# Cosine attention and an MLP mixer on one core: loading q and k of pairs 15 to 17 ahead of v of pairs 12 to 17, with the row transposes of u and the weight loads moved

## The chip, the cores and the metric

The kernel runs on one core of a Trainium2 chip. The metric is device time in microseconds (us). The engines are TensorE (PE in the profile; PEld are its weight loads), VectorE (DVE), ScalarE (ACT), GpSimd (POOL) and SyncE (SP), which here only issues DMAs.

## The reference

```python
batch, n_heads, seq, head_dim = (8, 12, 448, 64)
q_n = q / (np.linalg.norm(q, axis=-1, keepdims=True) + 1e-06)      # k_n likewise
scores = np.matmul(q_n, k_n.transpose(0, 1, 3, 2)) / tau            # tau = 0.1
attn = softmax(scores)
x = (attn @ v) as (8, 448, 768)                                     # heads side by side
h = np.maximum(x.T @ w_tok1, 0.0) @ w_tok2                          # w_tok1 448x256, w_tok2 256x448
u = x + h.T
h2 = np.maximum(u @ w_ch1, 0.0) @ w_ch2                             # w_ch1 768x1536, w_ch2 1536x768
return u + h2
```

Inputs and output are float32. The products are made in float16 with float32 sums.

## The kernel before, in words

**Units of work.** Two heads make a pair `p`; 6 pairs make a batch (`NPAIR`), so there are 48 pairs. Three pairs make a half `n` (`HP`), which is one load of q, of k and of v (576 KB each). The 448 rows are 384 main rows, three to a partition, and 64 rest rows. The rest rows (`xq`, `xk`, `xv`) are loaded for a whole batch in pieces of 256 bytes (192 KB for `xq`, twice 96 KB for `xk` and for `xv`).

**The path of a pair.** q and k are squared (`squares`, L176 on POOL or DVE, L174 on ACT), summed over the head (`sums`, L189, and `sums_x`, L193, on DVE), turned into reciprocal norms (`rnorms`, L197 to L200, on ACT) and scaled to float16 (`scaled`, L207, and `scaled_x`, L213 and L218, on POOL) into `kq`. PE transposes `kq` into `pst` (L239 to L244) for pairs below 15 and DVE copies it to `qk`; from pair 15 on (`DMA_FROM`) a transposing DMA does it (L261). PE makes the scores `psS` (L297) and `psX` (L304), ACT their exponentials `pt` (L298, L305), PE the product with v, `psO` (L318, L320), and DVE divides by the sums (L323, L324) into `x`. The token layer is `psR` (L338, relu on DVE L341) and `psU` (L357, with `x` added by PE at L362 or by DVE at L367); it gives a pair's 128 columns of u, transposed (`ut`). v is cast to float16 by `cast_v` (L164, L168).

**The channel layer.** When the sixth pair of a batch has been through the token layer, `ch_units` puts 12 units of the first product (`m_ch1`: six `psG` matmuls, L385, and a relu on ACT, L387) and 6 or 8 units of the second (`m_ch2`: twelve `psF` matmuls, L399, and on DVE the sum with u, L402) in a `queue`. `m_ch2` needs u with rows on partitions; `u_tpose` makes that by a transposing DMA for each pair (L376: `ur` from `ut`). `feed(budget, least)` takes units from the queue where the program calls it: it adds the budget to an account, takes units while the account covers half of the next one, and takes them against the account while less than `least` ns have been done. A unit's price in this account is its columns over 2.4.

**Order.** The whole order is written out by hand: a loop over slots `i`, one for each pair, issues loads, then scores, then sums and norms, scaling, squares, casts and weight loads, and then the rest of PE's work with calls of `feed` in between. The dictionaries `qk_at`, `v_at`, `x_at` (`xq`, `xk`), `xv_at` and `ut_at` say in which slot a load or a row transpose is issued; within a slot q and k come first, then `x`, v, `xv`, and then the transposes. All of these are issued by SP, one after the other; weights for the channel layer (`weights_ch1`, L154; `weights_ch2`, L158; 1152 KB each as float16) by POOL. Every engine works in order, so an instruction that waits holds all later ones of its engine. Slot 6 (`FIRST`) is the first slot after batch 0's attention; it also catches up two pairs of the token layer.

**Buffers.** `qm` and `km` have three tiles (halves), `vm` two, `xq`, `xk`, `xv` two (batches), the score tile `psS` two, the other PSUM tiles four in all, `ost` two, `ur` two. A load of half 5 into `qm` thus waits until pairs 6 to 8 (half 2) have been scaled.

Of the kernel before, what the change touches and what calls it, by code (L numbers as in the profile page):

```python
# [22 lines left out]
def kernel(  # L23
# [14 lines left out]
    B, H, S, E = q.shape  # L38
# [9 lines left out]
    DT = D // P  # L48
# [4 lines left out]
    NPAIR = H // 2  # L53
    NP_ALL = B * NPAIR
    HP = 3
    NHALF = 2 * B
# [48 lines left out]
    def load_q(n, g0=0, g1=6):  # L105
        nc.sync.dma_start(**main(qm, q, "qm", n, g0, g1))

    def load_k(n, g0=0, g1=6, eng=nc.sync):
        eng.dma_start(**main(km, k, "km", n, g0, g1))

    def load_v(n):
        nc.sync.dma_start(**main(vm, v, "vm", n, bufs=2))

    def load_xq(b, g0=0, g1=12):
        if b not in xq:
            xq[b] = qkv.tile([XR, H, E], FP32, name=f"xq_{b}", tag="xq", bufs=2)
        nc.sync.dma_start(out=xq[b][:, g0:g1], in_=q[b, g0:g1, SM:S].rearrange("g p e -> p g e"))  # L117
# [8 lines left out]
    def load_xk(b, g0=0, g1=12, eng=nc.sync):  # L126
        load_x2(xk, k, "xk", b, g0, g1, eng)

    def load_xv(b, g0=0, g1=12):
        load_x2(xv, v, "xv", b, g0, g1)  # L130
# [26 lines left out]
    def weights_ch2(i):  # L157
        nc.gpsimd.dma_start(out=wc2t[:, 6 * i:6 * i + 6, :],  # L158
                            in_=moe_w_ch2[768 * i:768 * (i + 1)].rearrange("(t p) d -> p t d", p=P))
# [89 lines left out]
    def tpose(p):  # L249
        pst = pst_tile(p)  # L250
        tpose_main(p, pst, 0)
        tpose_main(p, pst, 1)
        tpose_x(p, pst)
        return pst

    def qk_copy(p, pst):
        nc.vector.tensor_copy(out=qk_tile(p)[:, 0:P * 7 + XR], in_=pst[:, 0:P * 7 + XR])

    def dma_tpose(p):
        n, j = p // HP, p % HP  # L260
        nc.sync.dma_start_transpose(out=qk_tile(p)[:].rearrange("d (c s) -> d c s", c=8),  # L261
                                    in_=kqs[n % 2][:, j].rearrange("p a c e -> p (a c e)"))
# [66 lines left out]
    def x_tpose(p):  # L329
        xTs[p] = att.tile([P, (NC + 1) * P], FP16, name=f"xT_{p}", tag="xT")  # L330
        nc.sync.dma_start_transpose(out=xTs[p][:].rearrange("d (c s) -> d c s", c=NC + 1),
                                    in_=xs[p][:].rearrange("p c d -> p (c d)"))
# [37 lines left out]
    def u_tpose(p):  # L370
        b, dt = p // NPAIR, p % NPAIR
        odd = b % 2
        if b not in urt:
            urt[b] = mix.tile([P, DT, 4, P], FP16, name=f"ur16_{b}", tag="ur16")
        n, lo = NC + odd, SM * odd
        nc.sync.dma_start_transpose(out=urt[b][:, dt, 0:n], in_=pairt[b // 2][0][:, dt, lo:lo + P * n])  # L376
# [37 lines left out]
    def ns(cols, n=1):  # L414
        return n * cols / 2.4
# [6 lines left out]
    queue = []  # L422
    fed = [0.0]

    def feed(budget, least=0.0):
        fed[0] += budget
        done = 0.0
        while queue and (fed[0] > queue[0][0] / 2 or done < least):
            t, fn = queue.pop(0)
            fn()  # L430
            fed[0] -= t
            done += t

    def at(slots):
        got = {}
        for p, s in slots.items():
            got.setdefault(s, []).append(p)
        return got


    FIRST = NPAIR
# [8 lines left out]
            s = 1 + sq_slot[3 * n + (0 if c1 == 21 else 2)]  # L450
            rn_at.setdefault(s, []).append((n, c0, c1))
    sc_at = at({p: {7: 6}.get(p, p - 2 if p < DMA_FROM else p - 3) for p in range(3, NP_ALL)})
    early_qk = {2: 0, 3: 4, 4: 6, 5: 8}
    qk_at = at({n: early_qk.get(n, 3 * n - 8) for n in range(2, NHALF)})
    v_at = at({n: {2: 1, 3: 5}.get(n, 3 * n - 5) for n in range(2, NHALF)})
    x_at = at({b: {1: 0, 2: 6}.get(b, 6 * b - 8) for b in range(1, B)})
    xv_at = at({b: 6 * b - 5 for b in range(1, B)})
    cast_at = at({n: {1: 2, 2: 6}.get(n, 3 * n - 2) for n in range(1, NHALF)})
    tok_slot = {p: FIRST if p in (FIRST - 2, FIRST - 1) else p + 2 for p in range(NP_ALL)}
    tok_at = at(tok_slot)  # L460
    tok2_slot = {p: max(tok_slot[p] + (p in X_DMA), 3) for p in range(NP_ALL)}
    tok2_at = at(tok2_slot)
    ut_at = at({p: t + 1 for p, t in tok2_slot.items()})

    def norm_begin(p, eq, ek):
        squares(p, eq, ek)
# [3 lines left out]
    def norm_sums(p):  # L470
        sums(p)
        if p % HP == 0:
            sums_x(p // HP)
# [6 lines left out]
    with tc.manual_schedule():  # L480
# [77 lines left out]
        for i in range(NP_ALL + 2):  # L558
            for n in qk_at.get(i, ()):
                load_q(n)  # L560
                load_k(n)
            for b in x_at.get(i, ()):
                load_xq(b)
                load_xk(b)
            for n in v_at.get(i, ()):
                load_v(n)
            for b in xv_at.get(i, ()):
                load_xv(b)
            if DMA_FROM <= i + 2 < NP_ALL:
                dma_tpose(i + 2)  # L570
            if i - 2 in X_DMA:
                x_tpose(i - 2)
            for p in ut_at.get(i, ()):
                u_tpose(p)

            left = next((t + 1 - i for t in sorted(tok2_at) if t >= i + (i == FIRST) and
                         any(p % NPAIR == NPAIR - 1 for p in tok2_at[t])), 6)
            quota = max(sum(t for t, _ in queue) - 2000.0, 0.0) / (4 if FIRST <= i < FIRST + 3 else left)
            def next_qk(p):
                if p < min(DMA_FROM, NP_ALL):  # L580
                    qk_copy(p, tpose(p))

            def tok2(p):
                m_tok2(p)
                if p % NPAIR == NPAIR - 1:
                    queue.extend(ch_units(p // NPAIR))

            def norm_rn():
                for n, c0, c1 in rn_at.get(i, ()):
                    rnorms(n, c0, c1)  # L590

            if i == FIRST:
                m_tok1(i - 2)
                pv(i - 1, 0)
                pv(i - 1, 1)
                tok2(i - 2)
                m_tok1(i - 1)
                next_qk(i)
                tok2(i - 1)
                for p in sum_at[i]:  # L600
                    norm_sums(p)
                feed(0.0, 1000.0)
                score(i, 0)
                norm_rn()
                score(i, 1)
                feed(0.0, 2000.0)
            elif 0 < i < NP_ALL:
                score(i, 0, 2 if i < 4 else 0)
                score(i, 1)
            if i != FIRST:  # L610
                for p in sum_at.get(i, ()):
                    norm_sums(p)
                norm_rn()

            if i >= FIRST:
                for p in sc_at.get(i, ()):
                    norm_scale(p, nc.gpsimd)
            for p in sq_at.get(i, ()):
                norm_begin(p, nc.scalar if p < 18 else nc.gpsimd, nc.scalar if p == 3 else nc.vector if 9 <= p < 12 else nc.gpsimd)
            if i < FIRST:  # L620
                for p in sc_at.get(i, ()):
                    norm_scale(p, nc.gpsimd)
            for n in cast_at.get(i, ()):
                cast_v(n)
            if i in (2, 4):
                weights_ch1(i // 4)
            if i in (6, 7):
                weights_ch2(i - 6)

            if i < FIRST:  # L630
                if i:
                    pv(i - 1, 0)
                if i:
                    score(i, 2)
                    score_x(i)
                if i + 1 < FIRST:
                    next_qk(i + 1)
                for p in tok_at.get(i, ()):
                    m_tok1(p)
                if i:  # L640
                    pv(i - 1, 1)
                for p in tok2_at.get(i, ()):
                    tok2(p)
            elif i == FIRST:
                score(i, 2)
                score_x(i)
                feed(0.0, 1000.0)
                next_qk(i + 1)
                feed(0.0, 1000.0)
            else:  # L650
                feed(quota * 0.25)
                next_qk(i + 1)
                if i <= NP_ALL:
                    pv(i - 1, 0)
                for p in tok_at.get(i, ()):
                    m_tok1(p)
                feed(quota * 0.25, 400.0)
                if i < NP_ALL:
                    score(i, 2)
                    score_x(i)  # L660
                for p in tok2_at.get(i, ()):
                    tok2(p)
                feed(quota * 0.25)
                if i <= NP_ALL:
                    pv(i - 1, 1)
                feed(quota * 0.25)
            if i == 2:
                place_w2()
# [38 lines left out]
```

## Time and profile before

| | us |
|---|---|
| median of 5 runs | 414.63 |
| lowest, highest | 411.53, 2160.04 |
| the profiled execution's own time | 414.63 |
| its span, from first to last instruction | 412.8 |

Busy time in the span, by engine: PE 391.8 us, DVE 203.0, ACT 229.3, POOL 208.8. PE's time counts a matmul from its start to its modelled end, so a full PE is not PE at its peak: six psG matmuls in a row take 1.14 us in the chain of waits. PE's clock can be granted in part: the mean over the span was 0.98 of full speed.

Transfers: 67.51 MB in 137194 packets, of which 93184 are under 512 bytes (the rest rows and the transposes). SP's queue moved 61.36 MB of it, POOL's 5.18 MB. From its issue to its landing a load of q took 5.7 us in the median, of k 7.5, of v 7.1, a row transpose of u 2.8, half of a channel weight 13.1 to 13.4.

How to read it: a share of busy time is a mean over stages. The table by windows shows the stages, the timeline shows in brackets how long an engine sat idle before an instruction and what ended it, and SP's rows (SPq) are the time that SP needed to issue a DMA.

### The profile page before, as it was taken

The numbers are of one execution on the slowest core, as the hardware profiler recorded it, in microseconds if no ns is written. First come the engines' busy times: TensorE is split into PE (matmuls) and PEld (weight loads), VectorE is DVE, ScalarE is ACT, GpSimd is POOL, SyncE is SP. The second block draws the span as 40 slices with busy tenths as digits, with TensorE's granted clock in tenths as the row PEclk, the third lists the DMA queues.
The fourth block names the chain that finished last, engine by engine and source line by source line (L and its number), as shares of the span: only waits on it lengthen the run. The fifth ranks groups of instructions, "written<-read, shape, count | busy, mean of one in ns | idle before, by whom it ended". The sixth has DMA issues, their size and how long they took to land.

```text
span 412.8 us, 9115 instructions
## 1 busy us (share of the span) xinstructions
PE 391.8 (95%) x3646; PEld 227.2 (55%) x3646; DVE 203.0 (49%) x461; ACT 229.3 (56%) x415; POOL 208.8 (51%) x308
## 2 busy tenths in 40 slices
PE   7689989799999999999999998999999999999995
PEld 2356545466555564565555664555555565565562
DVE  5788656466544555445544555246453443243021
ACT  6997688654767446564666246564566435611400
POOL 5886477298193938576583908457491600000000
PEclk9899989899999999999999999899999999999998
DMA  8999999996997788989895898989782353013012
GB/s 219 272 234 202 231 232 189 257 179 203 174 229 109 218 149 220 206 188 197 232 191 74 235 131 218 179 150 235 171 151 49 87 146 65 15 51 104 2 75 77
DMA packets 137194, 67.51 MB, mean 164 GB/s; under 512 B 93184, under 2 KB 133568, under 8 KB 137152
## 3 DMA queue, kind: packets, MB, share of 16 engines
q1 hardware_dynamic: 132976, 61.36, 70.0%
q0 software_dynamic: 3632, 5.18, 7.4%
q8 instruction: 28, 0.46, 0.5%
q10 hardware_dynamic: 544, 0.39, 0.3%
q14 instruction: 14, 0.11, 0.1%
HBM read 43.38 MB, written 11.01 MB: 132 GB/s over the span
## 4 chain that ended last, share of the span: by engine, by line
PE 53%; POOL 19%; issue 12%; DMA 7%; SPq 4%; ACT 2%; DVE 2%; POOLq 0%; DVEq 0%; ACTq 0%
PE psF L399 18%; PE psG L385 16%; POOL kq L207 7%; POOL sq L176 6%; PE psO L318 5%; PE psS L297 4%; DMA xk<-in_k_dram 4%; PE psR L338 3%; DMA qm<-in_q_dram 3%; PE psU L357 3%; POOL sqx L176 2%; POOL kq L218 2%; PE psX L304 2%; SPq L117 2%; PE psO L320 1%
## 5 line engine op out<-in xcount | busy, mean ns | idle before, releaser
L298 ACT ACTIVATE pt<-psS 128x896 f16<-128x896 f32 x141 | 124.0, 914 | 73.3 <-PE psS L297 73.2
L385 PE MATMUL psG<-ut,wc1t 128*128 128x448 f16 x576 | 124.7, 358 | 0.0
L399 PE MATMUL psF<-wc2t,gt 128*128 128x384 f16 x672 | 118.0, 328 | 0.0
L387 ACT ACTIVATE gt<-psG 128x448 f16<-128x448 f32 x96 | 51.8, 544 | 77.8 <-PE psG L385 77.5
L207 POOL TENSOR_TENSOR kq<-km,rn 128x384 f16<-128x384 f32 x47 | 39.0, 830 | 101.5 <-ACT rn L200 90.3
L399 PEld LDWEIGHTS <-gt 128*128 128x128 f16 x672 | 63.8, 98 | 41.8 <-issue 3.8
L385 PEld LDWEIGHTS <-wc1t 128*128 128x128 f16 x576 | 53.2, 99 | 48.9 <-issue 8.3
L402 DVE TENSOR_TENSOR ost<-psF,ur 128x384 f32<-128x384 f32 x56 | 31.2, 558 | 84.1 <-PE psF L399 79.5
L318 PEld LDWEIGHTS <-pt 128*128 128x128 f16 x1152 | 52.7, 98 | 19.3 <-issue 8.5
L318 PE MATMUL psO<-vt,pt 128*128 128x65 f16 x1152 | 58.5, 195 | 2.8 <-ACT gt L387 2.8
L189 DVE TENSOR_REDUCE ssq<-sq 128x12 f32<-128x768 f32 (+1 forms) x49 | 45.1, 930 | 14.8 <-POOL sq L176 11.7
L297 PE MATMUL psS<-qk 64*128 64x448 f16 x282 | 44.4, 363 | 4.0 <-ACT pt L298 4.0
L324 DVE TENSOR_TENSOR x<-psO,rec 128x256 f16<-128x256 f32 x96 | 40.7, 424 | 3.3
L320 PE MATMUL psO<-vx,pt 128*128 128x130 f16 x192 | 42.3, 220 | 0.0
L323 DVE RECIPROCAL rec<-psO 128x4 f32<-128x4 f32 x96 | 17.1, 178 | 49.4 <-PE psO L320 49.1
L176 POOL TENSOR_TENSOR sq<-km 128x384 f32<-128x384 f32 x43 | 35.3, 823 | 11.6 <-DMA km<-in_k_dram 11.5
L207 POOL TENSOR_TENSOR kq<-qm,rn 128x384 f16<-128x384 f32 x47 | 38.9, 827 | 0.0
L338 PE MATMUL psR<-x,w1t 128*128 128x128 f16 x384 | 29.6, 220 | 0.1
L297 PEld LDWEIGHTS <-qk 64*128 64x128 f16 x282 | 10.7, 94 | 33.2 <-issue 29.5
L367 DVE TENSOR_TENSOR ut<-psU,xT 128x448 f16<-128x448 f32 (+2 forms) x39 | 17.6, 478 | 22.8 <-PE psU L357 17.1
L357 PE MATMUL psU<-w2t,r 128*128 128x448 f16 x96 | 26.0, 354 | 2.7 <-DVE x L324 2.6
L305 ACT ACTIVATE pt<-psX 128x448 f16<-128x448 f32 x48 | 26.0, 543 | 0.0
(75 smaller groups left out, 337.5 us busy)
## 6 DMA issues: line engine op xcount, KB each, us to landing
vm<-in_v_dram SPq DMA_DIRECT2D x16, 576.0 KB, 7.1
out_dram<-ost SPq DMA_DIRECT2D x24, 384.0 KB, 2.9
qm<-in_q_dram SPq DMA_DIRECT2D x15, 576.0 KB, 5.7
km<-in_k_dram SPq DMA_DIRECT2D x15, 576.0 KB, 7.5
wc1t<-in_moe_w_ch_dram POOLq DMA_DIRECT2D x2, 1152.0 KB, 13.4
wc2t<-in_moe_w_ch_dram POOLq DMA_DIRECT2D x2, 1152.0 KB, 13.1
out_dram<-ost SPq DMA_DIRECT2D x8, 192.0 KB, 3.0
xq<-in_q_dram SPq DMA_DIRECT2D x7, 192.0 KB, 8.7
```

The costliest lines, as they stand in the source:

```text
L176: eng.tensor_tensor(out=out, in0=src, in1=src, op=ALU.mult)
L189: nc.vector.tensor_reduce(out=ssqs[p // HP % 3][:, lo + 6 * a0:lo + 6 * a1], in_=sq[p][:, a0:a1].rearrange("p a g e -> p (a g) e"), axis=A ...
L207: eng.tensor_tensor(out=kqs[n % 2][:, j, a, 0:NC, :].rearrange("p c (g e) -> p g c e", g=2), in0=src, in1=_bcast_free(rn, E), op=ALU.mult)
L297: nc.tensor.matmul(psS[:, g, 0:S], qk[r, P * c:P * (c + 1)], qk[r, 512:512 + S], start=True, stop=True)
L298: nc.scalar.activation(out=pt[:, 2 * S * c:2 * S * (c + 1)].rearrange("p (g s) -> p g s", g=2), in_=psS[:, :, 0:S], func=AF.Exp, scale=inv ...
L318: nc.tensor.matmul(psO[:, mm, E1 * g:E1 * (g + 1)], pt[:, at:at + P], vt[:, 2 * j + g, c, 0:E1], start=(g == 0 and c == 0), stop=False)
L320: nc.tensor.matmul(psO[:, mm, :], pt[:, PX + lo:PX + lo + P], vx[:, j, 0:2 * E1], start=False, stop=True)
L324: nc.vector.tensor_tensor(out=xs[p][:, 2 * a:2 * a + 2, :].rearrange("p m (g e) -> p m g e", g=2), in0=o[:, :, :, 0:E], in1=_bcast_free(re ...
L338: nc.tensor.matmul(psR[:, tt, :], w1t[:, m, tt * P:(tt + 1) * P], xs[p][:, m, :], start=(m == 0), stop=(m == NC))
L385: nc.tensor.matmul(psG[:], wc1t[:, dt, ct * P:(ct + 1) * P], ut[:, dt, sp], start=(dt == 0), stop=(dt == DT - 1))
L387: nc.scalar.activation(out=gt[:, ct, sp], in_=psG[:], func=AF.Relu)
L399: nc.tensor.matmul(psF[:], gt[:, ct, lo:lo + P], wc2t[:, ct, dh * DH:(dh + 1) * DH], start=(ct == 0), stop=(ct == CT - 1))
```

## The change

Six edits, all of order:

- q and k of half 5 (pairs 15 to 17) are issued in slot 7 instead of 8; v of half 4 (pairs 12 to 14) in slot 9 instead of 7, of half 5 in slot 11 instead of 10.
- the rest rows of q and k of batch 3 in slot 11 instead of 10; those of v of batch 2 in slot 9 instead of 7.
- the row transposes of u: of batch 0, three in slot 8 and three in slot 9, instead of slots 4, 4, 5, 6, 7, 7; of batch 1, two each in slots 12, 13 and 14, instead of one each in slots 9 to 14. From batch 2 on they stay.
- the weights of the channel layer in slots 2, 5, 7 and 8 instead of 2, 4, 6 and 7.
- the budget of `feed` in slots 6 to 11: such that six units are left of the queue at slot 12, spread evenly.
- the last forced feed between the scores of slot 6: one unit (1000 ns) instead of two (2000 ns).

```diff
-    early_qk = {2: 0, 3: 4, 4: 6, 5: 8}
+    early_qk = {2: 0, 3: 4, 4: 6, 5: 7}
     qk_at = at({n: early_qk.get(n, 3 * n - 8) for n in range(2, NHALF)})
-    v_at = at({n: {2: 1, 3: 5}.get(n, 3 * n - 5) for n in range(2, NHALF)})
-    x_at = at({b: {1: 0, 2: 6}.get(b, 6 * b - 8) for b in range(1, B)})
-    xv_at = at({b: 6 * b - 5 for b in range(1, B)})
+    v_at = at({n: {2: 1, 3: 5, 4: 9, 5: 11}.get(n, 3 * n - 5) for n in range(2, NHALF)})
+    x_at = at({b: {1: 0, 2: 6, 3: 11}.get(b, 6 * b - 8) for b in range(1, B)})
+    xv_at = at({b: {2: 9}.get(b, 6 * b - 5) for b in range(1, B)})
...
-    ut_at = at({p: t + 1 for p, t in tok2_slot.items()})
+    ut_at = at({p: 8 + p // 3 if p < NPAIR else 12 + (p - NPAIR) // 2 if p < 2 * NPAIR else t + 1
+                for p, t in tok2_slot.items()})
...
-            quota = max(sum(t for t, _ in queue) - 2000.0, 0.0) / (4 if FIRST <= i < FIRST + 3 else left)
+            if FIRST <= i < 2 * NPAIR:
+                quota = max(len(queue) - 6, 0) * ns(S, DT) / (2 * NPAIR - i)
+            else:
+                quota = max(sum(t for t, _ in queue) - 2000.0, 0.0) / left
...
                 score(i, 1)
-                feed(0.0, 2000.0)
+                feed(0.0, 1000.0)
...
-            if i in (2, 4):
+            if i in (2, 5):
                 weights_ch1(i // 4)
-            if i in (6, 7):
-                weights_ch2(i - 6)
+            if i in (7, 8):
+                weights_ch2(i - 7)
```

## The prediction

> **What bounds the kernel now.** I read the page first: which engine is full, and what the chain of waits names.
>
> ```profile
> PE 391.8 (95%) x3646; PEld 227.2 (55%) x3646; DVE 203.0 (49%) x461; ACT 229.3 (56%) x415; POOL 208.8 (51%) x308
> ```
>
> TensorE (PE) has something in flight for 391.8 of 412.8 us; the others have half their time free. The matmul work is the same in both kernels, so time can only come from the 21 us in which PE stands, or from PE running at less than its full clock. The table of ten-us windows (columns: length, then busy time of PE, PEld, DVE, ACT, POOL, then granted clock, DMA share, GB/s) says where this lies. I leave out the first 40 us, where the order is not changed, and the last window.
>
> ```profile
> 50.00:60.00 10.00, 8.05 (x90) 4.79 (x89) 7.67 (x16) 9.81 (x23) 7.17 (x13) 0.94 1.17 249
> 70.00:80.00 10.00, 7.23 (x87) 4.58 (x85) 4.38 (x9) 5.70 (x12) 0.97 (x2) 0.96 1.19 206
> 160.00:170.00 10.00, 9.36 (x97) 5.42 (x95) 5.18 (x12) 6.47 (x11) 9.86 (x15) 1.00 1.07 245
> 250.00:260.00 10.00, 8.09 (x64) 4.30 (x64) 3.24 (x7) 4.93 (x8) 9.76 (x15) 0.84 0.87 204
> ```
>
> In the first, ACT is full (9.81): it is the limit there. In the second nothing is full: something is waited for. The timeline of PE gives the gaps (in brackets: idle time, and what ended it) and the cold matmuls after them.
>
> ```profile
> 56.17 0.36 PE L297 MATMUL psS<-qk 64*128 64x448 f16 x2 [1.22 <-ACT pt L298]
> 57.71 0.23 PE L243 MATMUL pst<-id,kq 128*128 128x128 f16 x1 [0.73 <-POOL kq L218]
> 59.12 2.45 PE L385 MATMUL psG<-ut,wc1t 128*128 128x448 f16 x6
> 63.90 1.31 PE L385 MATMUL psG<-ut,wc1t 128*128 128x448 f16 x6
> ...
> 79.07 0.40 PE L318 MATMUL psO<-vt,pt 128*128 128x65 f16 x6 [2.77 <-ACT gt L387]
> 80.81 3.00 PE L399 MATMUL psF<-wc2t,gt 128*128 128x384 f16 x12
> 85.22 2.11 PE L399 MATMUL psF<-wc2t,gt 128*128 128x384 f16 x12
> ```
>
> Why was ACT late at 79? The chain of waits has "DMA qm" (10.86 us) ending at 77.57, so I read ACT, POOL and SP's queue around it.
>
> ```profile
> 60.67 5.93 SPq L376 DMA_TRANSPOSE ur<-ut  x2
> 66.71 1.02 SPq L106 DMA_DIRECT2D qm<-in_q_dram  x1
> 121.55 1.20 SPq L376 DMA_TRANSPOSE ur<-ut  x1
> ...
> 77.66 0.52 ACT L174 ACTIVATE sq<-qm 128x384 f32<-128x384 f32 x1 [3.34 <-DMA qm<-in_q_dram]
> 79.47 0.82 POOL L176 TENSOR_TENSOR sq<-km 128x384 f32<-128x384 f32 x1 [9.03 <-DMA km<-in_k_dram]
> ```
>
> So q of pairs 15 to 17 is issued at 66.71 behind two row transposes of u that held SP for 5.93 us (1.20 each in calm water), lands 10.9 us later, and ACT, which works in order, holds the squares ahead of two relus whose PSUM tiles PE needs. The other gap, at slot 34:
>
> ```profile
> 256.43 0.69 PE L357 MATMUL psU<-w2t,r 128*128 128x448 f16 x2 [1.91 <-DVE x L324]
> 256.92 2.45 PE L385 MATMUL psG<-ut,wc1t 128*128 128x448 f16 x6
> ```
>
> There DVE waited (4.04 + 0.28 us) for POOL's squares, which POOL starts only after the scaling that the norms of slot 33 release; slot 33 was too short (6.07 us, 243.99 to 250.06) to cover POOL's 6.4 us.
>
> **What the Trainium skill says.** "TensorE: Matmul & The Clock Gate", Part 1: the array's clock falls to half after an idle activity window and needs a busy one (about 3.4 us) to return. The trace agrees on the half (psG unit 2.45 against 1.30), and shows that gaps of 1.22 + 0.73, of 2.77 and of 1.91 us were enough, while 0.64 us at 163.9 was not. "DMA: Bandwidth & Descriptors", Issuing engines are not separate DMA queues: SP's and POOL's transfers share the same 16 DMA engines. The trace agrees: while POOL's weight loads ran, q's and k's landings took 10.9 to 13.1 us; from 113 us on 4.5 to 6.2. "Perfetto Trace Analysis", What "DMA-bound" means, reads a solid issuing queue as descriptor generation; here the same transpose took SP 1.2 us or 3 to 4, so I read the surplus as back-pressure.
>
> **The change part by part.** No instruction is added or removed; what moves is the order on SP and POOL, and how psG (first channel layer, 1.14 us a unit in the chain of waits) and psF (second, 1.95 us) are dealt to the slots. Units per slot of batch 0's and 1's work, before: slot 6: 4 psG, 7: 1, 8: 1, 9: 3, 10: 2, 11: 2 psF, 12: 2 psF, 13: 1 psF. After: 3, 1, 1, 1, 1 psG, then 4 psG, 2 psF, 3 psF. Both have done 12 psG and 5 psF at the end of slot 13, so that is where I compare: before, slot 13 ends at 102.40.
>
> *SP's queue.* Moved past q and k of pairs 15 to 17: three issues of transposes (1.62 + 5.93 us, of batch 0), v of 12 to 14 (0.53) and xv (5.69). The new limit is the buffer: there are three qm tiles, and pair 8's scaling on POOL ends at 50.1 (49.28 + 0.83). So these loads are issued near 50 instead of 66.7, and with the worst landing seen (13.5 us) land by 64; ACT needs them near 71. The 2.77 us gap at 79 goes, with its cold clock: 0.9 (psF 3.00 for 2.11), 0.4 (psS 0.93 for 0.55), 0.3 in psO: 4.4 us in all.
>
> *What is late next.* v and xv of pairs 12 to 14 are issued near 60 and 61 instead of 54 and 55. At the landings of before (11.4 and 12.6 to 14.4) they are there at 72 and 75 to 79. POOL wants them at about 73, so it may wait 5 us; but what it then scales is wanted by PE only in slot 12, near 83. Covered. If that cover were gone, a late us costs a us.
>
> *Weights.* Same four issues of 0.9 us on POOL, one to two slots later. First psF is now after 80 and the seventh psG in slot 10 or 11, wc1's second half issued near 40 lands (13.4) by 54. Nothing. *Batch 1's transposes* from slot 12 are wanted by psF of slot 17. Nothing.
>
> *Lean slots.* A slot without units costs PE 3.8 us (slot 13: 5.76 less 1.95), with one psG 4.95; ACT took 5.16 for slot 7. So slots 7 to 10 are ACT's, and the gaps of 1.22 and 0.73 with the cold psG stay (slot 8's order is the same). Slot 7 starts at 50.2 instead of 50.66: the unit taken out is worth 1.14, but PE then meets pair 7's kq, ready at 48.5, some 0.7 too early. Slots 7 and 8 take what they took, 12.76: 63.0. Slots 9 and 10 at 5.2: 73.4. Slots 11 to 13 are PE's: 3.8 + 4 x 1.14 = 8.4; 3.8 + 2 x 1.95 = 7.7; 3.8 + 3 x 1.95 = 9.65. Sum 99.15, and 0.3 for small waits: 99.5. Gain 2.9 us; bounds 0 (the lean slots idle and run cold once more, 1.7, and ACT waits for POOL's sums, 1.2) and 6.5 (slot 8's cold spell goes as well).
>
> *Slots 33 and 34.* The carried budget shifts units: before, slot 33 had psF + 1 psG, after, psF + 3 psG, so slot 33 is 2.3 us longer and covers POOL. The gap of 1.91 goes, and with it 1.15 (psG) + 0.4 (psO twice 0.54 for 0.35): 3.4 us. Bounds 0 and 3.6. Slots 15 and 27 lose one psG each; they then hold 3 psG and psF + 2 psG, more than slot 21 (psF + 1 psG), whose stall was 0.64: at most 0.6, taken as nothing. Elsewhere PE is full, so what is won is kept.
>
> Sum: 2.9 + 3.4 = 6.3 us. The profiled execution took 414.63, which is its span of 412.8 and 1.8 around it, and is also the median of the runs shown. 414.63 - 6.3 = 408.3.
>
> **The rivals.** A measurement tells about 1% here, 4.1 us.
> (a) *Handed back.* The lean slots starve PE: it waits for ACT instead of q, and the clock drops again in slot 9 or 10; only the 2.77 us gap is exchanged. For: ACT 9.81 of 10 in the window 50 to 60. Against: its work per slot is 5.2 and PE's 4.95. With slots 33 and 34 unchanged too: gain 0 to 3, 413.
> (b) *Slower: SP stands.* q of 15 to 17 now waits in order for pair 8's scaling, with all later loads behind it. If SP reaches it at 40 and the rings run empty until 50, up to 10 us of DMA time is lost in a stage where DMA is full (share 1.17, 1.19). Then xk of pair 18 (in: 79.08, landed about 86) comes at 96 and POOL's squares end at 97.5, where DVE wants them in slot 13 near 91; DVE's blocked queue stalls PE 6.5 us plus a cold spell of 1.7. Less 2.9: +5.3, 419.9 (416.5 with the gain at slot 34). It decides once that xk lands after 91. Against: landings of 11 to 13 us at 41 say that the rings hold ten us of work, and wc1's second half runs meanwhile.
> (c) *Nothing in the DMA changes.* The stage stays full and q lands just as late: the gap shrinks to 1 to 2 us; 411 with slot 34, 414 without. Against: 16 us earlier in one queue.
> (d) *More.* Slot 8's cold spell goes too: 6.5 + 3.4, 404.7.
>
> **How the numbers follow.** Forecast (405.5 to 410.4) 0.50; (d) 0.08; (a) 0.14, (c) 0.10, both mostly within 1%; (b) 0.18, slower by over 1%. Faster by over 1%: 0.50 + 0.08 = 0.58; within: 0.24; slower: 0.18. The range takes in (a), (c), (d) and the lower part of (b): 403 to 416.5.
>
> **What would show it.** Right: q of pair 15 issued near 50, ACT's squares at about 71 with no wait for DMA, no PE gap before the first psF, slot 13's end near 99.5, no gap of over 1 us in slot 34. Wrong: SP idle before q with the DMA share falling below 0.8 there; new gaps "<- ACT pt" in slots 9 and 10; DVE waiting for POOL in slot 13; POOL waiting for DMA over 6 us at its cast of v.

## The result, and the profile after

| | kernel before | changed kernel |
|---|---|---|
| median, us | 415.19 (80 runs) | 408.63 (43 runs) |
| lowest, us | 406.76 | 407.73 |
| highest, us | 427.35, and one of 2160.04 | 411.13 |
| ratio of the times, 95% interval | | 0.997 (0.9952 to 0.9988) |

The ratio compares only executions within 1.5% of the fastest of their kernel, which are 22 of the 80 of the kernel before and all of the changed one. The executions of the kernel before spread over 20 us, those of the changed kernel over 3.4 us, and the profiled execution of before (414.63) was a middling one. So the change takes 1.6% off the median (408.63 / 415.19 = 0.984) and 0.3% off the best executions. The forecast was 408.3 from 414.63, 1.5% less. It hits the changed kernel's time. It hits the difference of the medians by luck, since the profile happened to be of a middling execution, and it misses how little the best executions of the two kernels differ.

The profile after (span 407.2 us, its own time 409.33), first the page's busy line:

```profile
PE 391.5 (96%) x3646; PEld 226.7 (56%) x3646; DVE 203.2 (50%) x461; ACT 228.3 (56%) x415; POOL 208.3 (51%) x308
```

The windows that answer to those of before (length, busy PE, PEld, DVE, ACT, POOL, granted clock, DMA share, GB/s):

```profile
50.00:60.00 10.00, 8.13 (x88) 5.12 (x85) 6.72 (x15) 8.80 (x20) 6.78 (x11) 0.86 1.10 230
70.00:80.00 10.00, 9.94 (x102) 5.75 (x100) 6.11 (x14) 9.29 (x23) 9.86 (x14) 1.00 1.17 248
160.00:170.00 10.00, 9.36 (x80) 4.77 (x78) 5.08 (x13) 5.76 (x10) 8.69 (x13) 1.00 1.16 231
250.00:260.00 10.00, 10.00 (x102) 5.57 (x101) 5.58 (x14) 6.98 (x11) 9.86 (x14) 1.00 1.07 260
```

Two of the four holes are filled: 70 to 80 (PE 7.23 before, 9.94 now) and 250 to 260 (8.09, now 10.00). PE's busy time in the windows 50 to 60 and 160 to 170 is as it was. PE's timeline shows the same two gaps there, a cold psG unit after them, a warm one later for the comparison, and in slot 34 a psU that no longer waits:

```profile
55.10 0.36 PE L297 MATMUL psS<-qk 64*128 64x448 f16 x2 [1.16 <-ACT pt L298]
56.62 0.23 PE L243 MATMUL pst<-id,kq 128*128 128x128 f16 x1 [0.71 <-POOL kq L218]
58.49 2.31 PE L385 MATMUL psG<-ut,wc1t 128*128 128x448 f16 x6
64.46 1.30 PE L385 MATMUL psG<-ut,wc1t 128*128 128x448 f16 x6
...
254.72 0.54 PE L357 MATMUL psU<-w2t,r 128*128 128x448 f16 x2
```

SP's queue, and the square on ACT that had waited 3.34 us for q of pair 15:

```profile
49.50 0.37 SPq L106 DMA_DIRECT2D qm<-in_q_dram  x1
50.80 3.95 SPq L376 DMA_TRANSPOSE ur<-ut  x3
54.85 0.54 SPq L112 DMA_DIRECT2D vm<-in_v_dram  x1
55.44 1.94 SPq L124 DMA_DIRECT2D xv<-in_v_dram  x2
...
71.00 0.51 ACT L174 ACTIVATE sq<-qm 128x384 f32<-128x384 f32 x1
```

q is issued at 49.50, when pair 8's scaling has freed its buffer, and lands 4.4 us later, 17 us before ACT squares it. Three transposes take 3.95 us where two had taken 5.93.

I took the start of each slot (its first score matmul on PE) from the traces. Both kernels do the same units of work in slots 6 to 18 (23 psG and 9 psF) and in slots 19 to 36 (36 psG and 20 psF):

| profile | before | before, second | before, third | after | after, second | after, third |
|---|---|---|---|---|---|---|
| slot 6 starts at | 44.31 | 43.53 | 43.92 | 43.67 | 44.02 | 44.67 |
| slots 6 to 18 take | 94.67 | 93.32 | 104.13 | 93.09 | 93.07 | 93.08 |
| slots 19 to 36 take | 138.21 | 135.68 | 137.13 | 134.80 | 136.20 | 134.80 |
| slot 37 to the end | 135.59 | 135.60 | 135.61 | 135.66 | 135.59 | 135.67 |
| span | 412.78 | 408.13 | 420.79 | 407.22 | 408.88 | 408.23 |

The second and third profiles are those of the experiments below. Against the profile that I had, the first one of the changed kernel wins 0.6 + 1.6 + 3.4 us, of which the 0.6 lie ahead of slot 6 and are no more than profiles of one kernel differ by there (43.67 to 44.67). Against the second profile of the kernel before it wins 0.9 us, and the second profile of the changed kernel, which lost 1.4 us in slots 35 and 36, wins nothing.

### The profile page after: what moved, and what is told of

The parts are those of the page before. It is cut to its first block, busy times and chain, and to the rows that moved or that the text cites. A ratio compares the mean times of both kernels' runs of the same rounds, so it can differ in the third digit from the quotient of the medians.

```text
span 407.2 us, 9113 instructions
## 1 busy us (share of the span) xinstructions
PE 391.5 (96%) x3646; PEld 226.7 (56%) x3646; DVE 203.2 (50%) x461; ACT 228.3 (56%) x415; POOL 208.3 (51%) x308
## 4 chain that ended last, share of the span: by engine, by line
PE 77%; ACT 7%; POOL 6%; DVE 5%; issue 4%; DMA 1%; SPq 0%; POOLq 0%; DVEq 0%
PE psF L399 24%; PE psG L385 24%; PE psO L318 7%; PE psS L297 7%; PE psR L338 4%; PE psU L357 4%; ACT pt L298 3%; PE psX L304 3%; PE psO L320 2%; POOL kq L207 2%; POOL sq L176 2%; DVE ssq L189 1%; DMA qm<-in_q_dram 1%; POOL kq L218 1%; POOL sqx L176 1%
```

## The experiments

Each median stands with its number of runs and its range. "Before" is the kernel before, run beside them on the same chip. The four groups ran on different chips or at different times, so a median is compared best with others of its group. All experiments but the unchanged kernels combine parts of the diff shown above; where there is another edit, it is shown.

**First four: does the gap belong to the kernel or to the execution, and which half of the change does the work?**

`before_again` has no edit.

> The kernel before, unchanged, to have a second profile of it and its spread on this chip. Theory 1 (the two gaps that the prediction removes, 2.77 us at slot 10 and 1.91 us at slot 34, are not in every execution: whether q of pairs 15 to 17 comes in time depends on how full the DMA rings are): times spread over several us; where this profile's span is near 407, the gap before the first psF is under 1 us and slot 34's under 1 us. Theory 2 (both gaps are in every execution, and the changed kernel pays the same sum elsewhere): both gaps again at 2.5 to 3 and 1.5 to 2 us, whatever the span.

415.89 us (6 runs, 407.15 to 421.35; the profiled one took 409.98). The second profile of the same program, PE:

```profile
55.38 0.37 PE L297 MATMUL psS<-qk 64*128 64x448 f16 x2 [1.21 <-ACT pt L298]
56.92 0.23 PE L243 MATMUL pst<-id,kq 128*128 128x128 f16 x1 [0.73 <-POOL kq L218]
58.16 1.30 PE L385 MATMUL psG<-ut,wc1t 128*128 128x448 f16 x6
64.55 0.37 PE L297 MATMUL psS<-qk 64*128 64x448 f16 x2 [3.13 <-ACT pt L298]
...
253.04 0.55 PE L357 MATMUL psU<-w2t,r 128*128 128x448 f16 x2 [0.64 <-DVE x L324]
```

and what ACT waited for:

```profile
62.75 0.52 ACT L174 ACTIVATE sqx<-xq 64x384 f32<-64x384 f32 x1 [3.89 <-DMA xq<-in_q_dram]
76.62 0.52 ACT L174 ACTIVATE sq<-qm 128x384 f32<-128x384 f32 x1 [1.35 <-DMA qm<-in_q_dram]
```

The gaps of slot 8 are there to a hundredth, but the psG unit behind them ran at the full clock ("warm"): 1.30. Slot 34's gap is 0.64 instead of 1.91. And another load is late: `xq` of batch 2, for slot 8, by 3.89 us, while q of pair 15 is late by 1.35 instead of 3.34. Theory 1 holds for slot 34; for the loads it was too narrow, since it knew only q of pairs 15 to 17.

What makes slot 34's gap 1.91 in one profile and 0.64 in the other can be read on DVE in slot 33. First the profile before, then this one:

```profile
245.89 0.56 DVE L402 TENSOR_TENSOR ost<-psF,ur 128x384 f32<-128x384 f32 x1 [3.07 <-DMA out_dram<-ost]
253.84 0.95 DVE L189 TENSOR_REDUCE ssq<-sq 128x12 f32<-128x768 f32 x1 [4.04 <-POOL sq L176]
...
241.97 0.56 DVE L402 TENSOR_TENSOR ost<-psF,ur 128x384 f32<-128x384 f32 x1 [1.27 <-PE psF L399]
250.44 0.95 DVE L189 TENSOR_REDUCE ssq<-sq 128x12 f32<-128x768 f32 x1 [2.79 <-POOL sq L176]
```

In the first, DVE waits for an output to leave the buffer `ost`, and its sums for the next norms start later; the norms, POOL's scaling and then POOL's squares hang on them. Counted from the start of slot 33, the squares come 1.27 us later than in the second profile, and so does PE. Seven profiles deal the units to slots 33 and 34 as before: the gap is 1.91 to 1.97 in the four in which DVE waits more than 3 us for that output, and 0.64 in the three in which it doesn't wait for it.

`dma_order_only`: the edits of loads, transposes and weights, none of feed.

> From the kernel before: only the order of loads, row transposes and weights is changed; feed keeps its budget and its 2000 ns. Theory 1: the gap for q at slot 10 is gone in every execution, so the spread narrows to 3 to 4 us as in the changed kernel, and its median lies 4 us or more under the median of before. Theory 2: median within 1 us of before, gaps of like size in other places.

408.25 us (6 runs, 406.39 to 409.25; before 413.15; ratio 0.990, 0.984 to 0.996), as theory 1 had it, and ACT and POOL wait for no load. What is late next is a weight, as PE's timeline shows; slot 34's gap is longer than in before's first profile, with a warm unit behind it:

```profile
77.79 1.14 PE L399 MATMUL psF<-wc2t,gt 128*128 128x384 f16 x6 [0.99 <-DMA wc2t<-in_moe_w_ch_dram]
...
251.82 0.55 PE L357 MATMUL psU<-w2t,r 128*128 128x448 f16 x2 [1.97 <-DVE x L324]
252.20 1.30 PE L385 MATMUL psG<-ut,wc1t 128*128 128x448 f16 x6
```

`feed_only`: the quota and the 1000 ns, all DMAs where they were.

> From the kernel before: only the budget of feed in slots 6 to 11 and the 1000 ns are changed; all DMAs stay where they were. Theory 1: q of pairs 15 to 17 is still issued behind two row transposes near 66, and PE reaches the need for it some 6 us sooner (slot 10 starts near 68), so the wait for DMA at ACT's squares is longer than before, 5 us or more, and the median is equal to that of before or up to 3 us above it; the spread stays wide. Theory 2: 3 us faster, since slot 34 no longer stalls.

421.53 us (6 runs, 417.44 to 425.05; ratio 1.019, 1.009 to 1.028), slower than either theory had it. SP, ACT and PE:

```profile
51.73 10.28 SPq L124 DMA_DIRECT2D xk<-in_k_dram  x2
...
71.46 0.52 ACT L174 ACTIVATE sqx<-xq 64x384 f32<-64x384 f32 x1 [12.44 <-DMA xq<-in_q_dram]
73.26 0.56 PE L297 MATMUL psS<-qk 64*128 64x448 f16 x2 [11.68 <-ACT pt L298]
```

The two issues of `xk` held SP for 10.28 us, and PE stood for 11.68 behind `xq`. The place was wrong in theory 1 (`xq`, not q), the direction right. Slots 19 to 36 took 134.96 us, as in the changed kernel.

`after_again` has no edit of the changed kernel.

> The changed kernel again, beside the others on the same chip. Theory 1: 407.5 to 411.5 in all executions. Theory 2: the same; it serves as the mark for the two halves of the change.

409.27 us (22 runs, 408.0 to 412.0; ratio 0.9975, 0.9950 to 0.9999). On the same chip the DMA order alone had 408.25: with it in place, the edits of feed gained nothing. In the profile of the DMA order alone slots 6 to 18 take 89.84 us, 3.2 less than in the changed kernel, and slots 19 to 36 137.08, 0.9 to 2.3 more.

**Second four: which DMA edit, and what do the feed edits cost?**

`transposes_only`: only `ut_at` as in the change.

> From the kernel before: only the row transposes of u of batches 0 and 1 move to slots 8, 9 and 12 to 14. Theory A (the transposes ahead of the loads of slots 5 to 8 are the cost; what is ahead of q of pairs 15 to 17 in slot 7 is small): the rest rows xq and xk of batch 2 are issued near 36 instead of 43 to 47 and land before 58, q of pairs 15 to 17 goes out near 56 and lands by 67, no wait for DMA on ACT or POOL between 50 and 90; median 408 to 409, spread 3 us. Theory B (the place of q ahead of v is what counts): a wait of 1 to 3 us for q at slot 10 stays, median 411 or more.

408.88 us (22 runs, 405.69 to 411.78; before 415.47, ratio 1.0003, 0.9961 to 1.0045). SP and POOL:

```profile
56.10 2.37 SPq L106 DMA_DIRECT2D qm<-in_q_dram  x1
61.45 13.76 SPq L376 DMA_TRANSPOSE ur<-ut  x6
73.68 0.82 POOL L176 TENSOR_TENSOR sq<-km 128x384 f32<-128x384 f32 x1 [4.13 <-DMA km<-in_k_dram]
```

q goes out at 56.10 and ACT waits for nothing; k still makes POOL wait 4.13 us, which PE doesn't feel. Moving the transposes by itself leaves 6 of the 20 us of spread; a gain over the best executions of before is not shown (the ratio). That is theory A, but for k and for twice the spread; `xq` and `xk` went out at 40.46 to 50.00, not near 36.

`loads_only`: only the loads of q, k, v, `x` and `xv`.

> From the kernel before: only q and k of pairs 15 to 17, v of 12 to 17, xq, xk of batch 3 and xv of batch 2 move; transposes and weights stay. Theory A: q of pairs 15 to 17 comes in time (issued near 56), but xq and xk of batch 2 are still behind the transposes of slots 4 and 5, so waits of 2 to 12 us for them at slot 8 to 9 stay in some executions; median 411 to 414, spread 8 us or more. Theory B: median within 1 us of 408.3, spread 3 us.

409.74 us (22 runs, 406.83 to 422.36; before 415.47, ratio 0.993, 0.989 to 0.997): nine of 22 runs take 414 or more, the others 407 to 412. The wide spread is what theory A foretold, whose range for the median was 411 to 414. Its reason, that the loads of slot 6 are still behind the transposes of slots 4 and 5, is likely but not shown: the profile caught a good execution (v of pairs 12 to 14 made POOL wait 6.3 us without harm to PE).

`dma_order_and_quota`: the changed kernel with `feed(0.0, 2000.0)` left as before.

> The changed kernel, but with the 2000 ns of feed between the scores of slot 6 as before: the budget of slots 6 to 11 is the new one. In the profiles so far, slots 6 to 8 take 18.7 us with 5 units in the changed kernel and 17.5 with 6 where only the DMA order is changed. Theory A (the unit taken out of slot 6 is what costs: PE meets kq of pair 7 too early, and slot 6 to 8 idle): slots 6 to 8 are back at 17.5 with 6 units, median 407.5. Theory B (the lean slots 9 and 10 cost): slots 9 and 10 are short of work for PE, at ACT's 5.2 us each with 3.8 + 1.1 of PE's, median 408.5 to 409.5, like the changed kernel.

406.62 us (6 runs, 405.82 to 408.58; ratio 0.989, 0.981 to 0.997). Slots 6 and 7 take 10.28 us with 5 psG units; in the changed kernel 9.91 with 4. So the unit taken out saved 0.37 us of its 1.14. From slot 8 to 13 the changed kernel, which has one unit more to do there, takes 1.66 more; from 14 to 18, at equal work, 0.71. The loss in slot 6 is as theory A has it, and the median 0.9 us under its forecast; its 17.5 us for slots 6 to 8 were not met (19.06, with a cold unit in slot 8), and that the loss goes on to slot 18 was in neither. The changed kernel's first profile shows where it goes on, on DVE and PE:

```profile
116.67 0.95 DVE L189 TENSOR_REDUCE ssq<-sq 128x12 f32<-128x768 f32 x1 [2.44 <-POOL sq L176]
119.60 0.55 PE L357 MATMUL psU<-w2t,r 128*128 128x448 f16 x2 [0.52 <-DVE r L341]
```

With 1000 ns in slot 6 the account of feed gives slot 15 three psG units, with 2000 ns four. The shorter slot doesn't cover POOL's squares, and PE waits 0.52 us in slot 16. All five profiles with 1000 ns have three units there and this wait, the thirteen with 2000 ns have four and don't.

`dma_order_slot33`: the DMA order alone, and the last feed of slot 33 forced:

```diff
-                feed(quota * 0.25)
+                feed(quota * 0.25, 3000.0 if i == 33 else 0.0)
```

> Only the DMA order is changed, and two psG units are moved from slots 34 and 36 to the end of slot 33. Theory A (the gap at slot 34 comes from a slot 33 too short to cover POOL's scaling and squares): the gap of 0.6 to 2 us at psU in slot 34 is gone, slots 33 to 36 take 1 to 2 us less than with the DMA order alone (23.5 us, one unit counted), median 406.5 to 407.5. Theory B (the gap is set by when the output DMA lands, whatever slot 33 holds): the gap stays, median 408.3.

408.36 us (22 runs, 406.67 to 412.57), no gain over the DMA order alone. PE:

```profile
79.58 0.64 PE L399 MATMUL psF<-wc2t,gt 128*128 128x384 f16 x2 [3.50 <-DMA wc2t<-in_moe_w_ch_dram]
254.99 0.55 PE L357 MATMUL psU<-w2t,r 128*128 128x448 f16 x2 [0.83 <-DVE x L324]
```

Its profile is one in which DVE waits for the output (3.17 us), so its gap of 0.83 is to be set against the 1.91 to 1.97 of the four others: both theories name a part, the output's landing adds to the gap and a longer slot 33 shortens it. In the changed kernel, which holds 3 psG in slot 34 too, psU waits for nothing, but none of its three profiles has so late an output (a wait of 2.05 us at most). That it fills the long gap is therefore not shown.

**Third four: the slot 6 unit, the cold clock, the weights.** `quota_again` is `dma_order_and_quota` once more. `quota_warm` adds eight matmuls on unused data in slot 8:

```diff
                 score(i, 0, 2 if i < 4 else 0)
+                if i == 8:
+                    busy(ps.tile([P, 512], FP32, name="warm_0", tag="b"), 5)
                 score(i, 1)
...
         tpose_main(p, pst, 1)
+        if p == 9:
+            busy(ps.tile([P, 512], FP32, name="warm_1", tag="b"), 3)
         tpose_x(p, pst)
```

> The changed kernel with 2000 ns instead of 1000 in slot 6 once more, beside the next three. Theory A (the unit that the changed kernel takes out of slot 6 costs it 2 us, which add up in slots 6 to 18): 406 to 407.5, 1.5 to 2.5 us under the changed kernel's 408.6 to 409.3. Theory B (the six executions measured so far were lucky): 408 to 409.

> As the one before it, with eight matmuls on unused data (0.2 us each) put into the two gaps of slot 8: five between its first scores, where PE waits 1.2 us for ACT, and three ahead of the last transposes of pair 9, where it waits 0.7 us for POOL. Theory A (the clock falls because PE stood idle there, in some executions): the cold psG unit after them (2.05 to 2.45 us instead of 1.30) is gone in the profile, granted clock 0.99 or more in all executions, the median 0.5 to 1.3 us under the kernel without them and the spread smaller. Theory B (the fall comes from elsewhere, or the added matmuls delay as much as they save): median equal or up to 1 us above.

407.13 us (6 runs, 405.81 to 408.46) without, 405.78 (6 runs, 405.50 to 411.22) with them. PE with them:

```profile
54.52 1.24 PE L232 MATMUL warm<-id 128*128 128x512 f16 x5 [0.40 <-ACT gt L389]
56.33 0.81 PE L232 MATMUL warm<-id 128*128 128x512 f16 x3
58.22 1.30 PE L387 MATMUL psG<-ut,wc1t 128*128 128x448 f16 x6
```

The unit is warm, but one profile can't show it, since that happens without them too.

`dma_order_f1000`: the DMA order and the 1000 ns, with the old quota. `loads_and_transposes`: these two alone, weights and feed as before.

> The DMA order of the changed kernel and the 1000 ns in slot 6, with the old budget of feed (which then hands out three psG units in slot 8 instead of one). Theory A (the unit missing in slot 6 leaves PE waiting for kq of pair 7 wherever the others go): slot 6 to 7 saves 0.3 to 0.4 us for one unit less, a wait of about 0.45 us at pst; median 408.5 to 410, 1 us or more above the DMA order alone (408.3). Theory B (only together with the new budget does it cost): 407.5 to 408.3.

409.07 us (6 runs, 408.39 to 414.97), 0.8 over the DMA order alone, which ran on another chip, with the wait for pair 7 that theory A names. Slots 6 and 7 save 0.37 us.

```profile
48.52 0.34 PE L239 MATMUL pst<-id,kq 128*128 128x128 f16 x3 [0.45 <-POOL kq L207]
```

> Loads and row transposes as in the changed kernel; the weights stay in slots 2, 4, 6 and 7, and feed stays. Theory A (with the old feed the later weights are what is late next: the DMA order alone showed a wait of psF for wc2 of 1.0 us, and of 3.5 us in the variant with slot 33): no wait of psF for wc2, median 407 to 408, spread at most 4 us. Theory B (moved weights are needed to let q of pairs 15 to 17 and the rest rows through): waits of over 1 us for q, k, xq or xk at slots 8 to 10, median 409 or more.

407.37 us (6 runs, 406.79 to 410.52; ratio 0.987, 0.983 to 0.992): psF doesn't wait for wc2, as theory A had it. On the same chip it is not told apart from `quota_again` (407.13), which also moves the weights and has the new budget.

**Last four, on one chip.**

> The changed kernel, on the same chip as the next two. Theory A (the unit taken out of slot 6 costs it 2 us): 408.5 to 409.5. Theory B (the 2 us between it and the variant with 2000 ns are those of other chips): within 0.7 us of the next kernel.

> The changed kernel with 2000 ns in slot 6. Theory A: 1.5 to 2.5 us under the changed kernel on this chip, 406.5 to 407.3, in the profile no wait for kq of pair 7 and no wait of psU for DVE's r in slot 16. Theory B: within 0.7 us of it.

> The same with the eight matmuls on unused data in slot 8. Theory A (the clock falls after the gaps of slot 8 in some executions): 0.5 to 1.3 us under the kernel without them, 405.5 to 406.3, and no cold psG in slot 8. Theory B: equal to it.

Changed kernel 409.38 us (6 runs, 408.08 to 410.33; ratio 0.989, 0.986 to 0.993); with 2000 ns 406.78 (405.55 to 410.59; ratio 0.984, 0.979 to 0.989); with the fillers 407.44 (406.06 to 407.84). So the unit taken out of slot 6 costs the changed kernel 2.6 us on one chip. The fillers gained 1.35 us on one chip and lost 0.66 on the other: their two profiles had no cold unit, a gain in time is not shown. With the fillers in, one profile had a wait of 4.08 us for an output in slot 33 and a gap of 1.33 us in slot 34. The profile with 2000 ns caught the run of 410.59, which shows what is late next, on POOL and PE:

```profile
74.11 1.14 POOL L164 CAST vt<-vm 128x1152 f16<-128x1152 f32 x1 [2.68 <-DMA vm<-in_v_dram]
...
83.49 2.40 PE L385 MATMUL psG<-ut,wc1t 128*128 128x448 f16 x6 [1.62 <-DVE qk L257]
```

> The kernel before once more, for a third profile of it. If the loss after a gap is a matter of the execution and not of the gap, this profile has the same gaps of 1.2 and 0.7 us in slot 8 and one of 0.6 to 2 us in slot 34, with or without a cold unit behind them, and its loads for slots 8 to 10 (xq, xk of batch 2; q, k of pairs 15 to 17) come late by amounts other than in the first two (0 and 3.3 us; 3.9 and 1.3 us on ACT). If it is a matter of the gap, all three have cold units at the same places.

415.39 us (22 runs, 410.14 to 422.63). Its profile is of the longest of them. SP, ACT, and then PE:

```profile
55.65 11.75 SPq L124 DMA_DIRECT2D xk<-in_k_dram  x2
...
72.64 0.52 ACT L174 ACTIVATE sqx<-xq 64x384 f32<-64x384 f32 x1 [9.57 <-DMA xq<-in_q_dram]
...
57.32 0.23 PE L243 MATMUL pst<-id,kq 128*128 128x128 f16 x1 [0.73 <-POOL kq L218]
58.56 1.30 PE L385 MATMUL psG<-ut,wc1t 128*128 128x448 f16 x6
74.45 0.56 PE L297 MATMUL psS<-qk 64*128 64x448 f16 x2 [12.63 <-ACT pt L298]
```

The same gaps in slot 8 (1.22 at 55.78, 0.73 at 57.32), and a warm unit again; a wait of 12.63 us at slot 9, where the first profile had none; in slot 34 a gap of 1.93 with a warm unit. How late a load is, and whether the clock falls, belongs to the execution.

## Why the prediction was right or wrong

**What held.** q of pair 15 issued "near 50" (49.50), ACT's squares "at about 71" (71.00) without a wait, no PE gap before the first psF, no gap in slot 34; POOL didn't wait for v (5.5 us to landing, not 11). Slots 7 to 10 took 23.14 us where I had 23.2. Slot 13's end came "near 99.5" (99.48) by luck: slot 6 began 0.64 us earlier than in the profile of before, and the slots in between took 0.6 more than forecast. Rival (a) shows in none of the three profiles (no wait for ACT in slots 9 and 10). Nor did (b) and (c) come: SP stood 3.4 us before q, but the DMA share was 1.17 from 40 to 50, and xk of pair 18 had landed by 82. Slots 19 to 36 won 3.41 us against the profile of before, where the forecast had 3.4; this too is partly luck, as the next part shows.

**What failed: the base of the sum.** "414.63 - 6.3 = 408.3" sets what one execution lost as what the kernel loses. The second profile has 0.78 us where the gap of 2.77 was (and one of 3.13 at slot 9), 0.64 where 1.91 was, and no cold unit behind any gap, for which I had counted 1.6 and 1.5 us. In it slots 6 to 18 took 93.32 and slots 19 to 36 135.68, so against this execution the terms are 0.2 and 0.9 us, not 2.9 and 3.4; their sum is 0.3% of the time, which agrees with the ratio of the best executions. I had even said that the median of the runs shown agreed; that only says that it was a middling one of a wide spread.

The same holds of the cause that I gave for slot 34. A slot 33 too short to cover POOL is in all seven profiles with that dealing of units, and the gap that they all have is 0.64 us. The other 1.27 us of the 1.91 were an output that left its buffer late in four of the seven.

**What was not seen.** The chain of waits of before named `xk` of batch 2 with 11.27 us, ending in a wait of 0.30 us on POOL (first the chain, then POOL's timeline):

```profile
51.75 11.27 DMA xk<-in_k_dram
63.15 0.51 POOL L176 TENSOR_TENSOR sqx<-xk 128x192 f32<-128x192 f32 x1 [0.30 <-DMA xk<-in_k_dram]
```

I passed it over as met in time. In the second and third profiles the same load made POOL wait 1.62 and 2.19 us, and `xq`, issued ahead of it, made ACT wait 3.89 and 9.57. The row transposes are the part of the change with the largest effect on the median: moved alone, they bring it from 415.47 to 408.88. In the sum I had only those that stood ahead of q of pairs 15 to 17, not those of slots 4 and 5, which stand ahead of `xq` and `xk`.

**What was mis-sized.** *Lean slots*: for slots 6 to 13 I expected 55.2 us (99.5 - 44.31) and the changed kernel took 55.81, since slot 13 needed 10.40 for 9.65. The 0.7 us handed back at the end of slot 6 were right (0.77). *Slot 15*, which loses a psG unit, "at most 0.6, taken as nothing": it cost a wait of 0.52 us in slot 16 in each of the changed kernel's three profiles, and slots 14 to 18 took 37.28 us for 36.58. With 2000 ns in slot 6 this wait is absent, and the kernel is 1.5 to 2.8 us faster (medians of 406.62 to 407.13 against 408.63 to 409.38). Against the DMA order with the old feed, which takes 53.26 us for the same work in slots 6 to 13, the changed kernel's dealing is a loss of 2.5 us (1.0 of it the cold unit in slot 8); with 2000 ns it is even (53.33 in `quota_again`). *Weights*, priced at nothing: right beside the new quota, wrong without it (0.99 and 3.50 us of waiting for wc2). *Clock*: the Trainium skill ("TensorE: Matmul & The Clock Gate", Part 1) ties the fall to an idle activity window of about 3.4 us that runs free of the kernel, and I made a fixed price of it; of three profiles of before with the same two gaps, 1.95 us together, one had a cold unit behind them. So less idle time than the page says can be enough, and needn't be. *A reading*: from 113 us on the loads of q and k landed after 4.4 to 9.2 us, not 4.5 to 6.2; this changes no term.

A better version than the changed kernel is the change without the 1000 ns: medians of 406.62, 407.13 and 406.78 us on three occasions, against 408.6 to 409.4 for the changed kernel and 413 to 415 for the one before. The loads and transposes alone were not told apart from it on the one chip where both ran (407.37 and 407.13).

What stays open: why the loads and outputs of one execution land later than those of the next, whether fillers in slot 8 pay, and whether the changed dealing of slots 33 and 34 also fills the gap that a late output makes.

## What to carry to other kernels

Before a sum is made against a profile, ask whether its losses are the kernel's or the execution's: look at the spread of the times, take a second profile of the unchanged kernel, and price only what both show. A load that lands just in time is a loss waiting for another execution; look at slack, not only at waits. And a queue that issues DMAs one after the other should hold first what is needed first: transposes that nobody reads for 50 us (issued at 31 and 33 in the first profile, first read on DVE at 83.85) belong behind the loads.

## What the runs showed of the hardware

The time that SP needs to issue the same DMA varied with the place and the execution: a row transpose took 1.2 us late in the kernel, 2.3 on the mean (13.76 / 6) between 61 and 75 us in `transposes_only`, and a single one 7.65 us in before's third profile; two issues of `xk` took from 2.3 to 11.75 us.

PE's clock did not fall behind every gap of the same length. Sixteen profiles have the gaps of 1.2 and 0.7 us in slot 8; the psG unit behind them took 2.05 to 2.45 us in eight of them and 1.30 in the other eight. Behind a gap of 1.9 to 2.0 us in slot 34 the clock fell in two profiles and not in two others.
